# Running the value matmuls of an attention stage as pairs of 64-row matmuls

## The chip, the cores and the metric

The kernel runs on one core of a Trainium2 chip. The metric is the device time of one execution in microseconds; lower is better. The core's engines work side by side, each through its own instructions in order: TensorE (PE, with its weight loads as PEld), VectorE (DVE), ScalarE (ACT), GpSimd (POOL) and SyncE (SP, which here only issues DMAs). They wait for each other by semaphores.

## The reference

There are two stages. The first is an attention without softmax, over 8 batches of 3008 rows with 256 columns, and a key width of 64; the second a feed-forward layer with a cosine gate over the 24064 rows of the first one's result.

```python
scores = (1 / 3008) * z @ z.T             # per batch: [3008, 3008], z is [3008, 64]
attn   = maximum(scores, 0) ** 2
x      = u * (attn @ v)                   # u, v: [3008, 256]
h      = x.reshape(24064, 256) @ w_in     # w_in: [256, 2048]
out    = (h * cos(h)) @ w_out             # w_out: [2048, 256]
```

Everything enters and leaves in float32.

## The kernel before, in words

Inputs are loaded with a cast to float16 (`emit_in_dma`, DMAs issued by POOL). `z` is stored twice side by side, so that its transpose `zTt` holds the same 64 rows in partitions 0 to 63 and 64 to 127. The factors 1/S are taken out of the first stage and put into the second.

**First stage.** The unit of work is a slot: one block of 256 query columns (`IB`, 12 blocks per batch, the last with 192) against four key blocks of 128 rows (`JPG` = 4). A batch has 12 x 6 = 72 slots, the whole stage 576. Slot `s` does the following.

- Scores (L233): four matmuls with a contraction over 64 rows into `scp`, two PSUM banks wide. They come in pairs, one on partitions 0 to 63 and one on 64 to 127, each half of the array with its own bank. `ps_sc` has two such tiles, so the scores of slot s+2 need the relu of slot s.
- Relu from PSUM into `rt` (L245 on ACT for 15 slots of 20, L247 on DVE for the other 5, which follow one another), then the square into `at` (L251 on DVE for 13 of 20, L255 on POOL for 7). Which engine takes which is a fixed pattern in the slot number.
- Values (L271), five slots later (`LAG_SLOTS` = 5): for each of the four key blocks and each half `nh` of the 256 value columns a matmul with a contraction over all 128 key rows, `v16` as the weights and `at` as the moving operand, into `oacc`. One `oacc` tile is one PSUM bank: both `nh` halves of a query block, 2 x 256 float32 columns. It collects six slots; `ps_acc` has two of them.
- After the sixth slot, x is formed (L282): for each `nh`, DVE multiplies the accumulator by the transposed `u` (`uTt`) into `xst`, which SP sends to a DRAM scratch `xT_dram`. There are 96 such query blocks.

Between the slots stand side jobs for the next batch (`side_items_for`): groups of up to eight 128 x 128 transposes of `z` (L137) and of `u` (L152) on PE into a bank `tps` of the pool `ps_tp` (two banks), each copied to SBUF by DVE or ACT in turn (L128, L130), nine groups per batch.

**Second stage.** Blocks of 512 rows: `hps` (L317), cosine on ACT (L325), product on DVE (L328), `ops` (L344), copy on ACT (L351), DMA out. It begins when the first has ended.

The order on each engine is that of a list scheduler that places the instructions at build time, with priorities and the free buffers of the pools in view. What is written later in the program can so stand earlier on an engine, where a buffer is free; a tile from a pool with no free buffer waits for the release of the oldest one.

Of the kernel before, what the change touches and what calls it, by code (L numbers as in the profile page):

```python
# [10 lines left out]
FP16 = mybir.dt.float16  # L11
FP32 = mybir.dt.float32


def _cdiv(a, b):
    return (a + b - 1) // b
# [3 lines left out]
def kernel(  # L20
# [9 lines left out]
    nc = tc.nc  # L30
    AF = mybir.ActivationFunctionType
    ALU = mybir.AluOpType

    B, S, D = u.shape
    dqk = z.shape[2]
    Dff = moe_w_in.shape[1]
    NTOK = B * S
    P = 128

    NJ = _cdiv(S, P)  # L40
    S_pad = NJ * P
    JLAST = S - (NJ - 1) * P
    NDH = _cdiv(D, P)
    NFT = _cdiv(Dff, P)

    IBW = 256
    IB = [(o, min(IBW, S - o)) for o in range(0, S, IBW)]
    JPG = 4
    TPG = 8
# [26 lines left out]
    with tc.tile_pool(name="a_in", bufs=2) as inpool, \  # L76
# [4 lines left out]
            tc.tile_pool(name="a_r", bufs=4) as rpool, \  # L81
            tc.tile_pool(name="a_a", bufs=8) as apool, \
            tc.tile_pool(name="ps_sc", bufs=2, space=bass.MemoryType.PSUM) as ps_sc, \
            tc.tile_pool(name="ps_acc", bufs=2, space=bass.MemoryType.PSUM) as ps_acc, \
            tc.tile_pool(name="ps_tp", bufs=2, space=bass.MemoryType.PSUM) as ps_tp:

        z16s, u16s, v16s, zTs, uTs = {}, {}, {}, {}, {}

# [35 lines left out]
        def tp_copy(dst, src):  # L124
            nonlocal tp_cnt
            tp_cnt += 1
            if tp_cnt % 2 == 0:
                nc.vector.tensor_copy(dst, src)  # L128
            else:
                nc.scalar.copy(dst, src)  # L130

        def emit_tp_z(bb, j0):
            z16 = z16s[bb]
            npk = min(TPG, NJ - j0)
            tps = ps_tp.tile([P, TPG * P], FP16, name="tps")
            for k in range(npk):
                nc.tensor.matmul(  # L137
                    tps[:, k * P:(k + 1) * P],
                    z16[:, j0 + k, :],
                    id16,  # L140
                    is_transpose=True,
                    start=(k == 0),
                    stop=(k == npk - 1),
                )
            tp_copy(zTs[bb][:, j0 * P:(j0 + npk) * P], tps[:, 0:npk * P])

        def emit_tp_u(bb, dh, j0):
            u16 = u16s[bb]
            npk = min(TPG, NJ - j0)
            tps = ps_tp.tile([P, TPG * P], FP16, name="tps")  # L150
            for k in range(npk):
                nc.tensor.matmul(  # L152
                    tps[:, k * P:(k + 1) * P],
                    u16[:, j0 + k, dh * P:(dh + 1) * P],
                    id16,
                    is_transpose=True,
                    start=(k == 0),
                    stop=(k == npk - 1),
                )
            tp_copy(uTs[bb][:, dh, j0 * P:(j0 + npk) * P], tps[:, 0:npk * P])  # L160

        def side_items_for(bb):
            items = []
            nb = bb + 1
            if nb < B:
                if nb >= 2:
                    items.append(lambda n=nb: alloc_zT(n))
                    items.append(lambda n=nb: alloc_uT(n))
                for j0 in range(0, NJ, TPG):
                    items.append(lambda n=nb, j=j0: emit_tp_z(n, j))  # L170
                for dh in range(NDH):
                    for j0 in range(0, NJ, TPG):
                        items.append(lambda n=nb, d=dh, j=j0: emit_tp_u(n, d, j))
                if nb + 1 < B:
                    items.append(lambda n=nb + 1: emit_in_dma(n))
            return items
# [7 lines left out]
        for j0 in range(0, NJ, TPG):  # L184
            emit_tp_z(0, j0)
        alloc_uT(0)
        for dh in range(NDH):
            for j0 in range(0, NJ, TPG):
                emit_tp_u(0, dh, j0)
# [12 lines left out]
        accs = {}  # L202
# [5 lines left out]
        for s in range(nslots + LAG_SLOTS):  # L208
            if s < nslots:
                b, gi, j0 = slots[s]  # L210
                if b != prev_b:
                    prev_b = b
                    while side_q:
                        side_q.pop(0)()
                    items = side_items_for(b)
                    nsb = len(IB) * (NJ // JPG)
                    every = max(1, nsb // (len(items) + 1)) if items else nsb
                    side_tick = 0
                    side_q = items
                    side_every = every  # L220
                side_tick += 1
                if side_q and (side_tick % side_every == 0):
                    side_q.pop(0)()
                ioff, iw = IB[gi]
                ztb = zTs[b]
                scp = ps_sc.tile([P, JPG * IBW], FP32, name="scp")
                nblk = (JPG * IBW * 4) // 2048
                per_blk = JPG // nblk
                for kk in range(per_blk):
                    for blk in range(nblk):  # L230
                        k = blk * per_blk + kk
                        r0 = blk * dqk
                        nc.tensor.matmul(  # L233
                            scp[:, k * IBW:k * IBW + iw],
                            ztb[r0:r0 + dqk, (j0 + k) * P:(j0 + k + 1) * P],
                            ztb[r0:r0 + dqk, ioff:ioff + iw],
                            start=(kk == 0),
                            stop=(kk == per_blk - 1),
                        )
                rt = rpool.tile([P, JPG, IBW], FP16, name="rt")  # L240
                at = apool.tile([P, JPG, IBW], FP16, name="at")
                scv = scp.rearrange("p (k w) -> p k w", k=JPG)
                ew_cnt += 1
                if (ew_cnt * 7919) % 20 < RELU_ACT_OF20:
                    nc.scalar.activation(rt[:, :, 0:iw], scv[:, :, 0:iw], AF.Relu)  # L245
                else:
                    nc.vector.tensor_scalar(  # L247
                        rt[:, :, 0:iw], scv[:, :, 0:iw], 0.0, None, ALU.max
                    )
                if (ew_cnt * 104729) % 20 < SQ_DVE_OF20:  # L250
                    nc.vector.tensor_tensor(  # L251
                        at[:, :, 0:iw], rt[:, :, 0:iw], rt[:, :, 0:iw], ALU.mult
                    )
                else:
                    nc.gpsimd.tensor_tensor(  # L255
                        at[:, :, 0:iw], rt[:, :, 0:iw], rt[:, :, 0:iw], ALU.mult
                    )
                ring[s] = at
            s2 = s - LAG_SLOTS
            if s2 >= 0:  # L260
                b2, gi2, j0_2 = slots[s2]
                ioff2, iw2 = IB[gi2]
                v16 = v16s[b2]
                if j0_2 == 0:
                    accs[(b2, gi2)] = ps_acc.tile([P, NDH * IBW], FP32, name="oacc")
                acc = accs[(b2, gi2)]
                at2 = ring.pop(s2)
                for k in range(JPG):
                    jj = j0_2 + k
                    for nh in range(NDH):  # L270
                        nc.tensor.matmul(  # L271
                            acc[:, nh * IBW:nh * IBW + iw2],
                            v16[:, jj, nh * P:(nh + 1) * P],
                            at2[:, k, 0:iw2],
                            start=(jj == 0 and nh == 0),
                            stop=(jj == NJ - 1 and nh == NDH - 1),
                        )
                if j0_2 + JPG >= NJ:
                    uT16 = uTs[b2]
                    xst = xpool.tile([P, NDH, IBW], FP16, name="xst")  # L280
                    for nh in range(NDH):
                        nc.vector.scalar_tensor_tensor(  # L282
                            xst[:, nh, 0:iw2],
                            acc[:, nh * IBW:nh * IBW + iw2],
                            1.0,
                            uT16[:, nh, ioff2:ioff2 + iw2],
                            ALU.mult,
                            ALU.mult,
                        )
                    del accs[(b2, gi2)]  # L290
                    for nh in range(NDH):
                        nc.sync.dma_start(
                            xT_dram[nh, :, b2 * S + ioff2:b2 * S + ioff2 + iw2],
                            xst[:, nh, 0:iw2],
                        )
# [99 lines left out]
```

## Time and profile before

| | |
|---|---|
| device time, median of 2 runs | 1498.08 us (1497.26 to 1498.9) |
| span of the profiled execution | 1495.1 us |
| TensorE clock granted, mean | 0.992 of full |
| PE, DVE, ACT, POOL busy, share of the span | 97%, 72%, 65%, 31% |
| first value matmul of the stage | 26.8 us |
| last x formed (L282) | 829.6 us |

The profile is that of one execution. A time of its own is not given beside its span; the median of the runs lies 3.0 us above the span, which is what lies around the first and the last instruction. The page has the busy time of each engine, the chain of work that ended last (followed back from the end, with the share of each line in it) and groups of instructions with their mean durations. Answers of the trace add the instructions in order of time (start and duration in us; a row joins several of one kind, "x4"), and who waited for whom. [...]matmuls that follow each other overlap in the records; what counts is the distance between their starts.

### The profile page before, as it was taken

Reading aid. Unit: us, or ns where it says so; the run is one execution under the profiler, and the core shown is the slowest. Engines: PE = TensorE matmul, PEld = TensorE weight load, DVE = VectorE, ACT = ScalarE, POOL = GpSimd, SP = SyncE. Lnnn points to the kernel's source line nnn. Section 1 sums busy time; section 2 is a strip of 40 time slices with the busy share of each in tenths; the row PEclk is TensorE's granted clock in tenths of the full one; section 3 lists DMA queues with packets and bytes.
Section 4 is the critical chain, followed back from the end, with each engine's and each line's share of the span. In section 5 each row is a group of like instructions: output and inputs, shape, how many; then the busy total and the mean of one; then the engine's idle time right before and its main releaser. Section 6 shows DMA issues by size and latency. Waiting matters only on the chain.

```text
span 1495.1 us, 29453 instructions
## 1 busy us (share of the span) xinstructions
PE 1443.2 (97%) x12000; PEld 953.8 (64%) x12000; DVE 1075.4 (72%) x1524; ACT 975.8 (65%) x1409; POOL 467.4 (31%) x274
## 2 busy tenths in 40 slices
PE   3799999999999999999999999999999999999998
PEld 2566666666666666666666666666666666666666
DVE  2487976877878878778677767667667667667664
ACT  1546566566565565665656877777777777778775
POOL 4565655656565554555555000000000000000000
PEclk9799999999999999999999999999999999999999
DMA  9990716434346250000100121121121111111111
GB/s 167 155 129 19 80 20 96 38 59 61 34 67 70 42 74 19 15 18 17 30 19 19 35 64 50 57 64 50 57 63 52 57 60 54 57 59 56 57 57 51
DMA packets 165001, 84.09 MB, mean 56 GB/s; under 512 B 55809, under 2 KB 164609, under 8 KB 164865
## 3 DMA queue, kind: packets, MB, share of 16 engines
q0 software_dynamic: 99616, 32.90, 20.5%
q1 hardware_dynamic: 65248, 49.30, 10.9%
q8 instruction: 94, 1.54, 0.4%
q14 instruction: 43, 0.34, 0.1%
HBM read 78.12 MB, written 36.96 MB: 77 GB/s over the span
## 4 chain that ended last, share of the span: by engine, by line
PE 82%; DVE 10%; DMA 2%; ACT 2%; issue 2%; POOL 0%; DVEq 0%; POOLq 0%; ACTq 0%
PE oacc L271 27%; PE hps L317 22%; PE ops L344 22%; PE scp L233 10%; DVE rt L247 5%; DVE at L251 4%; ACT rt L245 2%; DMA u_122<-in_u_dram 2%; DVE xst L282 1%; PE tps L152 1%; DMA u_106<-in_u_dram 1%; PE tps L137 0%; DVE uTt L128 0%; POOL z_100 L93 0%; ACT uTt L130 0%
## 5 line engine op out<-in xcount | busy, mean ns | idle before, releaser
L245 ACT ACTIVATE rt<-scp 128x1024 f16<-128x1024 f32 (+1 forms) x431 | 429.2, 1006 | 286.6 <-PE scp L233 270.7
L255 POOL TENSOR_TENSOR at<-rt 128x1024 f16<-128x1024 f16 (+1 forms) x202 | 398.5, 1978 | 322.4 <-ACT rt L245 165.7
L251 DVE TENSOR_TENSOR at<-rt 128x1024 f16<-128x1024 f16 (+1 forms) x374 | 372.8, 1006 | 156.6 <-ACT rt L245 154.1
L233 PE MATMUL scp<-zTt 64*128 64x256 f16 (+1 forms) x2304 | 224.5, 273 | 11.0 <-DVE rt L247 8.7
L317 PEld LDWEIGHTS <-w_in_65 128*128 128x128 f16 x1504 | 147.0, 98 | 70.3 <-issue 9.1
L247 DVE TENSOR_SCALAR rt<-scp 128x1024 f16<-128x1024 f32 (+1 forms) x145 | 168.6, 1193 | 1.9 <-PE scp L233 1.7
L351 ACT ACTIVATE osb<-ops 128x256 f32<-128x256 f32 x188 | 71.7, 382 | 147.9 <-PE ops L344 147.9
L233 PEld LDWEIGHTS <-zTt 64*128 64x128 f16 x2304 | 70.1, 94 | 123.9 <-issue 117.0
L282 DVE SCALAR_TENSOR_TENSOR xst<-oacc,uTt 128x256 f16<-128x256 f32 x192 | 74.8, 409 | 12.0 <-PE oacc L271 12.0
L271 PE MATMUL oacc<-at,v_110 128*128 128x256 f16 (+1 forms) x576 | 74.4, 272 | 0.5 <-DVE at L251 0.5
L271 PE MATMUL oacc<-at,v_5547 128*128 128x256 f16 (+1 forms) x576 | 74.2, 272 | 0.0
L271 PE MATMUL oacc<-at,v_6949 128*128 128x256 f16 (+1 forms) x576 | 74.1, 272 | 0.0
L271 PE MATMUL oacc<-at,v_4145 128*128 128x256 f16 (+1 forms) x576 | 74.1, 272 | 0.0
L271 PE MATMUL oacc<-at,v_1341 128*128 128x256 f16 (+1 forms) x576 | 74.1, 272 | 0.0
L271 PE MATMUL oacc<-at,v_2743 128*128 128x256 f16 (+1 forms) x576 | 74.1, 272 | 0.0
L271 PE MATMUL oacc<-at,v_126 128*128 128x256 f16 (+1 forms) x576 | 73.9, 272 | 0.0
L271 PE MATMUL oacc<-at,v_8351 128*128 128x256 f16 (+1 forms) x576 | 73.2, 272 | 0.0
L271 PEld LDWEIGHTS <-v_110 128*128 128x128 f16 x576 | 50.1, 98 | 19.9 <-issue 15.3
L271 PEld LDWEIGHTS <-v_1341 128*128 128x128 f16 x576 | 49.9, 98 | 19.4 <-issue 14.9
L271 PEld LDWEIGHTS <-v_6949 128*128 128x128 f16 x576 | 49.9, 98 | 19.4 <-issue 14.9
L271 PEld LDWEIGHTS <-v_2743 128*128 128x128 f16 x576 | 49.9, 98 | 19.4 <-issue 14.9
L271 PEld LDWEIGHTS <-v_4145 128*128 128x128 f16 x576 | 49.9, 98 | 19.4 <-issue 14.9
(1767 smaller groups left out, 2559.0 us busy)
## 6 DMA issues: line engine op xcount, KB each, us to landing
out_dram<-osb SPq DMA_DIRECT2D x47, 512.0 KB, 2.9
xT_dram<-xst SPq DMA_DIRECT2D x176, 64.0 KB, 1.6
u_106<-in_u_dram POOLq DMA_DIRECT2D x1, 1472.0 KB, 12.7
v_110<-in_v_dram POOLq DMA_DIRECT2D x1, 1472.0 KB, 18.5
u_122<-in_u_dram POOLq DMA_DIRECT2D x1, 1472.0 KB, 23.4
v_126<-in_v_dram POOLq DMA_DIRECT2D x1, 1472.0 KB, 25.7
u_1337<-in_u_dram POOLq DMA_DIRECT2D x1, 1472.0 KB, 14.3
v_1341<-in_v_dram POOLq DMA_DIRECT2D x1, 1472.0 KB, 16.3
```

Of the source, the lines that this page charges most:

```text
L152: nc.tensor.matmul(tps[:, k * P:(k + 1) * P], u16[:, j0 + k, dh * P:(dh + 1) * P], id16, is_transpose=True, start=(k == 0), stop=(k == npk ...
L233: nc.tensor.matmul(scp[:, k * IBW:k * IBW + iw], ztb[r0:r0 + dqk, (j0 + k) * P:(j0 + k + 1) * P], ztb[r0:r0 + dqk, ioff:ioff + iw], start= ...
L245: nc.scalar.activation(rt[:, :, 0:iw], scv[:, :, 0:iw], AF.Relu)
L247: nc.vector.tensor_scalar(rt[:, :, 0:iw], scv[:, :, 0:iw], 0.0, None, ALU.max)
L251: nc.vector.tensor_tensor(at[:, :, 0:iw], rt[:, :, 0:iw], rt[:, :, 0:iw], ALU.mult)
L255: nc.gpsimd.tensor_tensor(at[:, :, 0:iw], rt[:, :, 0:iw], rt[:, :, 0:iw], ALU.mult)
L271: nc.tensor.matmul(acc[:, nh * IBW:nh * IBW + iw2], v16[:, jj, nh * P:(nh + 1) * P], at2[:, k, 0:iw2], start=(jj == 0 and nh == 0), stop=( ...
L282: nc.vector.scalar_tensor_tensor(xst[:, nh, 0:iw2], acc[:, nh * IBW:nh * IBW + iw2], 1.0, uT16[:, nh, ioff2:ioff2 + iw2], ALU.mult, ALU.mult,)
L317: nc.tensor.matmul(hps[:, 0:tw], w_in16[:, k, ft * P:(ft + 1) * P], xt[:, k, 0:tw], start=(k == 0), stop=(k == NDH - 1),)
L344: nc.tensor.matmul(ops[0:m, :], gt[:, ft, tsub * P:tsub * P + m], w_out16[:, ft, :], start=(ft == 0), stop=(ft == NFT - 1),)
L351: nc.scalar.activation(osb[0:m, tsub, :], ops[0:m, :], AF.Copy, bias=0.0, scale=inv_s2,)
```

## The change

The value matmuls are split in two along the contraction. The half `h` = 0 multiplies key rows 0 to 63 of a block and `h` = 1 rows 64 to 127, each into an accumulator bank of its own, so a slot has 16 value matmuls of 64 rows in place of 8 of 128. When x is formed, ACT copies the first accumulator to SBUF (`s0`, float32), DVE adds the second from PSUM (`s1`, float32), and DVE multiplies the sum by `uTt`; each of the three takes both `nh` halves at once (128 x 512). The two pools `ps_acc` and `ps_tp`, two banks each, become one pool `ps_m` of four banks that both accumulators and the transposes draw from.

```diff
@@ -81,8 +81,8 @@
             tc.tile_pool(name="a_r", bufs=4) as rpool, \
             tc.tile_pool(name="a_a", bufs=8) as apool, \
             tc.tile_pool(name="ps_sc", bufs=2, space=bass.MemoryType.PSUM) as ps_sc, \
-            tc.tile_pool(name="ps_acc", bufs=2, space=bass.MemoryType.PSUM) as ps_acc, \
-            tc.tile_pool(name="ps_tp", bufs=2, space=bass.MemoryType.PSUM) as ps_tp:
+            tc.tile_pool(name="a_s", bufs=2) as spool, \
+            tc.tile_pool(name="ps_m", bufs=4, space=bass.MemoryType.PSUM) as ps_m:
 
         z16s, u16s, v16s, zTs, uTs = {}, {}, {}, {}, {}
 
@@ -132,7 +132,7 @@
         def emit_tp_z(bb, j0):
             z16 = z16s[bb]
             npk = min(TPG, NJ - j0)
-            tps = ps_tp.tile([P, TPG * P], FP16, name="tps")
+            tps = ps_m.tile([P, TPG * P], FP16, name="tps", tag="m")
             for k in range(npk):
                 nc.tensor.matmul(
                     tps[:, k * P:(k + 1) * P],
@@ -147,7 +147,7 @@
         def emit_tp_u(bb, dh, j0):
             u16 = u16s[bb]
             npk = min(TPG, NJ - j0)
-            tps = ps_tp.tile([P, TPG * P], FP16, name="tps")
+            tps = ps_m.tile([P, TPG * P], FP16, name="tps", tag="m")
             for k in range(npk):
                 nc.tensor.matmul(
                     tps[:, k * P:(k + 1) * P],
@@ -262,31 +262,41 @@
                 ioff2, iw2 = IB[gi2]
                 v16 = v16s[b2]
                 if j0_2 == 0:
-                    accs[(b2, gi2)] = ps_acc.tile([P, NDH * IBW], FP32, name="oacc")
+                    accs[(b2, gi2)] = [
+                        ps_m.tile([P, NDH * IBW], FP32, name="oacc", tag="m")
+                        for _ in range(2)
+                    ]
                 acc = accs[(b2, gi2)]
                 at2 = ring.pop(s2)
                 for k in range(JPG):
                     jj = j0_2 + k
                     for nh in range(NDH):
-                        nc.tensor.matmul(
-                            acc[:, nh * IBW:nh * IBW + iw2],
-                            v16[:, jj, nh * P:(nh + 1) * P],
-                            at2[:, k, 0:iw2],
-                            start=(jj == 0 and nh == 0),
-                            stop=(jj == NJ - 1 and nh == NDH - 1),
-                        )
+                        for h in range(2):
+                            r0 = h * dqk
+                            nc.tensor.matmul(
+                                acc[h][:, nh * IBW:nh * IBW + iw2],
+                                v16[r0:r0 + dqk, jj, nh * P:(nh + 1) * P],
+                                at2[r0:r0 + dqk, k, 0:iw2],
+                                start=(jj == 0 and nh == 0),
+                                stop=(jj == NJ - 1 and nh == NDH - 1),
+                            )
                 if j0_2 + JPG >= NJ:
                     uT16 = uTs[b2]
                     xst = xpool.tile([P, NDH, IBW], FP16, name="xst")
-                    for nh in range(NDH):
-                        nc.vector.scalar_tensor_tensor(
-                            xst[:, nh, 0:iw2],
-                            acc[:, nh * IBW:nh * IBW + iw2],
-                            1.0,
-                            uT16[:, nh, ioff2:ioff2 + iw2],
-                            ALU.mult,
-                            ALU.mult,
-                        )
+                    s0 = spool.tile([P, NDH, IBW], FP32, name="s0")
+                    s1 = spool.tile([P, NDH, IBW], FP32, name="s1")
+                    a0 = acc[0].rearrange("p (k w) -> p k w", k=NDH)
+                    a1 = acc[1].rearrange("p (k w) -> p k w", k=NDH)
+                    nc.scalar.copy(s0[:, :, 0:iw2], a0[:, :, 0:iw2])
+                    nc.vector.tensor_tensor(
+                        s1[:, :, 0:iw2], a1[:, :, 0:iw2], s0[:, :, 0:iw2], ALU.add
+                    )
+                    nc.vector.tensor_tensor(
+                        xst[:, :, 0:iw2],
+                        s1[:, :, 0:iw2],
+                        uT16[:, :, ioff2:ioff2 + iw2],
+                        ALU.mult,
+                    )
                     del accs[(b2, gi2)]
                     for nh in range(NDH):
                         nc.sync.dma_start(
```

In the changed file the value matmuls stand at L276, the copy at L290, the sum at L291 and the product at L294; lines up to L262 are where they were.

## The prediction

> **What bounds the kernel now.** I read the page first: the engine shares, then the chain that ended last.
>
> ```profile
> PE 1443.2 (97%) x12000; PEld 953.8 (64%) x12000; DVE 1075.4 (72%) x1524; ACT 975.8 (65%) x1409; POOL 467.4 (31%) x274
> ...
> PE oacc L271 27%; PE hps L317 22%; PE ops L344 22%; PE scp L233 10%; DVE rt L247 5%; DVE at L251 4%; ACT rt L245 2%; DMA u_122<-in_u_dram 2%; DVE xst L282 1%; PE tps L152 1%; DMA u_106<-in_u_dram 1%; PE tps L137 0%; DVE uTt L128 0%; POOL z_100 L93 0%; ACT uTt L130 0%
> ```
>
> TensorE carries the chain, and 38% of the span on it (oacc 27, scp 10, tps 1) is in the attention stage, up to about 830 us. The second stage (hps, ops) is untouched. But DVE rt and DVE at are on the chain too, with 9%: VectorE is second in line. The timeline of TensorE shows the rhythm of a slot (columns: start, duration, what):
>
> ```profile
> 403.95 0.39 PE L233 MATMUL scp<-zTt 64*128 64x256 f16 x4
> 404.27 1.05 PE L271 MATMUL oacc<-at,v_2743 128*128 128x256 f16 x8
> 405.25 0.39 PE L233 MATMUL scp<-zTt 64*128 64x256 f16 x4
> 405.58 1.05 PE L271 MATMUL oacc<-at,v_2743 128*128 128x256 f16 x8
> 406.46 0.61 PE L152 MATMUL tps<-id_58,u_4141 128*128 128x128 f16 x8
> ```
>
> A slot is 1.30 us. One matmul is recorded at 275 ns, so the eight full ones (1.05) start (1.05 - 0.275) / 7 = 0.11 us apart. The four 64-row ones end after 0.39: their last start is at 0.39 - 0.275 = 0.115, so two ran together, then two more, one step of 0.115 apart. Ten steps of 0.109 would make 1.09; the other 0.21 lies where the kinds meet: last scp start 404.07 to first oacc 404.27, and last oacc start 405.05 to next scp 405.25, 0.20 each instead of 0.11. The view of waits counts the same gaps on the weight loads:
>
> ```profile
> PEld L271 <- issue: 118.1, 569, 0.7
> PEld L233 <- issue: 117.0, 540, 2.0
> ...
> PE scp L233 <- DVE rt L247: 8.7, 19, 2.0
> ```
>
> About 0.21 per gap, once per slot each way, with no releaser that the profile knows; and TensorE hardly waits for VectorE (8.7 us in all). So changing between full and half matmuls costs about 0.2 us x 576 slots = 115 us, and the elementwise engines are just fast enough for 1.30. How just, the timeline of VectorE shows where five slots in a row have their relu on it (L247):
>
> ```profile
> 564.15 0.69 DVE L251 TENSOR_TENSOR at<-rt 128x1024 f16<-128x1024 f16 x1 [0.39 <-ACT rt L245]
> 564.76 2.35 DVE L247 TENSOR_SCALAR rt<-scp 128x1024 f16<-128x1024 f32 x2
> 567.02 0.68 DVE L251 TENSOR_TENSOR at<-rt 128x1024 f16<-128x1024 f16 x1
> 567.62 1.22 DVE L247 TENSOR_SCALAR rt<-scp 128x1024 f16<-128x1024 f32 x1
> 568.76 0.41 DVE L282 SCALAR_TENSOR_TENSOR xst<-oacc,uTt 128x256 f16<-128x256 f32 x1
> 569.09 0.92 DVE L251 TENSOR_TENSOR at<-rt 128x1024 f16<-128x1024 f16 x1
> 569.93 0.41 DVE L282 SCALAR_TENSOR_TENSOR xst<-oacc,uTt 128x256 f16<-128x256 f32 x1
> 570.26 2.34 DVE L247 TENSOR_SCALAR rt<-scp 128x1024 f16<-128x1024 f32 x2
> ```
>
> From 564.15 to 572.60 VectorE is never idle, and TensorE waits there once for 0.53 us. This stretch sets what a faster TensorE is worth.
>
> **What the Trainium skill says.** "TensorEngine Tiling (Array Packing)", section "Key Properties", says that changing the tiling mode drains the engine, and that tiles of one mode run in parallel: the trace agrees, with 0.20 instead of 0.11 us at each change and the four scp matmuls in 0.39. "PSUM — Partial Sum Buffer", section "Specifications (TRN2)", says that a VectorE instruction takes at most one tensor input from PSUM; hence the copy of one half to SBUF before the sum; nothing in this trace tests it. "SBUF — State Buffer", section "Who interferes with whom", says that a VectorE instruction with two SBUF inputs contends with GpSimd reading SBUF. The trace agrees: the squares (L251, two SBUF inputs) take 0.68 alone but 1.03 on average, the relus (one PSUM input) 1.21 always.
>
> **The change, part by part.** Instruction order is from the two built programs. Profiled span 1495.1, median of the runs 1498.1: I add 3.0 us to any span.
>
> TensorE. Per slot 8 full matmuls become 8 pairs of halves. Both kinds are now 64-row, so the two changes of mode go and the slot is ten steps: 1.10 at 0.110 a step. Its bounds are 1.09, and 1.20 if every pair takes the 0.115 to 0.12 seen at a first step. That is 0.20 x 576 = 115 us off, if nothing else is late. The 72 groups of 8 transposes stay full matmuls; each used to add 0.45 (with oacc before it in the same mode) and now brings two changes: 0.65, or +14 us.
>
> Start. Before, the nine transpose groups of batch 1 all stand ahead of the second value slot, and TensorE waits for loads from 29 to 56 us:
>
> ```profile
> 28.75 0.39 PE L233 MATMUL scp<-zTt 64*128 64x256 f16 x4
> 42.68 2.80 PE L137 MATMUL tps<-id_58,z_116 128*128 128x128 f16 x24 [13.54 <-DMA z_116<-in_z_dram]
> 50.29 1.89 PE L152 MATMUL tps<-id_58,u_122 128*128 128x128 f16 x16 [4.81 <-DMA u_122<-in_u_dram]
> ...
> 55.86 1.26 PE L271 MATMUL oacc<-at,v_110 128*128 128x256 f16 x10
> ```
>
> With one shared pool of four banks only the first group stands there; the value matmuls can go on at 43.5. That is 12 us won, 8 x 0.65 = 5 paid later: -7.
>
> x, 96 times. Out: two L282 of 0.41, VectorE 0.82. In: on ScalarE a copy 128x512, 0.60 by the line through 256 columns (0.382, L351) and 1024 (1.02, L245). On VectorE the sum from PSUM, 512 columns: 0.69 from 0.41 at 256 and 1.21 at 1024. Then a product of two SBUF inputs at one element a cycle: 0.69 by the same slope; "VectorE: DVE Perf Modes" prices an fp32 two-tensor sum of 512 at 691 ns. Beside GpSimd up to 1.36 (the mean of squares wholly beside it); I take 0.95. VectorE gets 1.64 for 0.82 each, +79 us in all; ScalarE +57. Two instructions overlap by some 0.08, which I take off below.
>
> The relu stretch. Let the first score matmul of the five VectorE slots start at 0, with the next wanted at 1.10, 2.20 and so on. The square ahead of the first relu waits for the last ScalarE relu: -1.10 + 0.39 + 1.02, then 0.6, so VectorE starts at about 1.0. The new order is relu, square, relu, relu, square, sum, relu, product, relu: 1.14 + 0.60 + 2.28 + 0.95 + 0.54 + 1.14 + 0.70 + 1.14 (sum and product weighted by how often they fall inside), and 0.15 for a transpose copy. That ends at 9.65. Scores have two buffers, so the seventh score matmul waits for the fifth relu: six slots take 9.7. Before they took 6 x 1.30 + 0.45 + 0.4 = 8.65 (563.96 to 572.83 in this piece: 8.87).
>
> The other 14 of 20 slots. ScalarE does 0.93 a relu, 2.3 copies of 0.5 for the sum, one transpose copy: 1.07 a slot; TensorE 1.10; with their jitter 1.12. 14 x 1.12 = 15.7, and 1.75 transposes x 0.65 = 1.1.
>
> Bank waits. The accumulators take two of four banks and a transpose takes the third, so after a transpose a new pair needs a bank of the pair that has just ended. In the built order 26 of 96 groups wait there for the copy on ScalarE (about 0.6 after the next scores) and 12 for the sum on VectorE (about 1.4); 26 x 0.6 + 12 x 1.4 = 32 us. Behind that matmul stand TensorE's next slots. A third falls in the relu stretch, where TensorE is late anyway; 0.7 per 20 slots remain.
>
> Sum per 20 slots: before 20 x 1.303 + 2.5 x 0.45 + 0.4 = 27.6; after 9.7 + 15.7 + 1.1 + 0.7 = 27.2. Times 28.5 such cycles: -11; start -7: -18. 1498.1 - 18 = **1480**. So the 115 us are nearly all given back: what is late next is VectorE's relu stretch, then the bank waits.
>
> **Rivals.**
> 1. Clearly faster: the stretch stays at 8.65 (sum and product fall in VectorE's idle time) and bank waits vanish in it: 8.65 + 14 x 1.10 + 1.1 = 25.15; -2.45 x 28.5 - 7 = -77: 1421. For it: VectorE is at 75 to 84% in the windows of this stage. Against: the built order puts the sum and product between the relus.
> 2. Slower, by the pairs themselves: 64-row pairs are seen only two in a row at full clock, with half the instructions per us that ten need. Two weight loads a pair, not hidden, make a step longer. Every 0.01 in a step costs 0.1 x 14 x 28.5 = 40 us in the 14 slots alone; from 0.122 on the kernel is slower than before by 2%. At 0.14 (slot 1.40): +56 for the slots, +14 transposes, +15 bank waits, -11 waits gone, -7 start: 1565. Against: both halves of a pair load within 0.11 us in scp.
> 3. Slower, by VectorE: GpSimd's squares cover the stretch, every square and product takes 1.36: +1.6 per cycle, +46: 1526.
>
> **How the numbers follow.** Forecast 0.45 (own range 1455 to 1510), first rival 0.20, second 0.15, third 0.20. Range 1425 to 1550, leaving out the far ends of the first and second. A measurement here tells about 2% (1468 to 1528). Faster: the first rival and the forecast's low edge, 0.28; slower: the larger part of the second and third, 0.27; same 0.45.
>
> **What would show it.** Right: no issue gaps left between scp and oacc, slots of 1.10 where ScalarE does the relus, a large wait of scp for DVE rt (some 40 us or more, from 8.7), a wait of oacc for the copy and the sum, value matmuls running by 44 us, L294 near 0.95. Wrong: steps of over 0.115 in the pairs; scp waiting for VectorE no more than before; a slot still at 1.30.

## The result, and the profile after

The changed kernel takes 1511.0 us (median of 2 runs, 1510.67 to 1511.33) against 1498.08: a ratio of 1.0089, with a 95% interval of 1.006 to 1.0118. It is slower, by less than 2% but beyond the noise; the forecast was 1480, a gain. The profiled execution spans 1508.8 us (1495.1 before). TensorE's granted clock was lower in it (mean 0.977, against 0.992), but the other run of the changed kernel had 0.986 and took no less (1511.33), so the clock doesn't look like the cause.

First the page of the changed kernel: engine shares, then the chain that ended last.

```profile
PE 1370.6 (91%) x16608; PEld 1076.0 (71%) x16608; DVE 1202.3 (80%) x1524; ACT 1008.9 (67%) x1505; POOL 475.9 (32%) x274
...
PE hps L327 22%; PE ops L354 22%; PE oacc L276 12%; DVE at L251 10%; DVE rt L247 9%; ACT rt L245 4%; PE scp L233 4%; DVE xst L294 3%; DVE s L291 2%; DMA z<-in_z_dram 2%; DMA u<-in_u_dram 1%; PE tps L152 1%; PE tps L137 0%; ACT s L290 0%; DVE uTt L128 0%
```

The second stage still holds 44% of the chain. In the first one the chain has moved: the value matmuls fall from 27% to 12%, and VectorE (at, rt, xst, s) rises from 10% to 24%. The view of waits says where the two meet:

```profile
PEld L233 <- issue: 110.3, 111, 2.6
...
PE scp L233 <- DVE rt L247: 88.4, 90, 2.4
...
PEld L276 <- issue: 15.9, 16, 2.9
...
PE oacc L276 <- DVE at L251: 9.2, 6, 2.7
...
PE oacc L276 <- ACT s L290: 1.3, 1, 1.3
```

The 0.21 us gaps between scores and values, 569 and 540 before, are down to 16 and 111. Those that are left are longer (110.3 us for the 111): most of them lie beside the waits of the score matmuls, the others at transposes. From the last score matmul to the first value matmul the median step is now 0.09 us, and back again 0.11, where both were 0.20. In place of the gaps the score matmuls wait 88.4 us for VectorE's relus, 8.7 before. The timeline of TensorE shows both kinds of slot:

```profile
406.61 0.38 PE L233 MATMUL scp<-zTt 64*128 64x256 f16 x4
406.83 1.04 PE L276 MATMUL oacc<-at,v 64*128 64x256 f16 x16
407.77 0.40 PE L233 MATMUL scp<-zTt 64*128 64x256 f16 x4
407.99 1.05 PE L276 MATMUL oacc<-at,v 64*128 64x256 f16 x16
409.63 0.39 PE L233 MATMUL scp<-zTt 64*128 64x256 f16 x4 [0.59 <-DVE rt L247]
...
424.00 0.38 PE L233 MATMUL scp<-zTt 64*128 64x256 f16 x4
424.21 1.04 PE L276 MATMUL oacc<-at,v 64*128 64x256 f16 x16
425.09 0.38 PE L233 MATMUL scp<-zTt 64*128 64x256 f16 x4
425.31 1.04 PE L276 MATMUL oacc<-at,v 64*128 64x256 f16 x16
426.18 0.38 PE L233 MATMUL scp<-zTt 64*128 64x256 f16 x4
```

Undisturbed, a slot is 1.09 us (424.00 to 425.09 to 426.18): ten steps of 0.109. The score matmul at 409.63 is one of those held up by a relu on VectorE.

**A measure used below.** The trace has all 2304 score matmuls, four to a slot, so each slot has a start. For the 27 whole cycles of 20 slots behind the first I averaged two pieces of time: from the first of the five slots with VectorE relus over six slots ("six"), and the other fourteen ("rest"). Lateness is the time from the start of that first slot to VectorE's first relu; its mean takes in the last cycle too, which is cut short.

| kernel | time us | six us | rest us | lateness us |
|---|---|---|---|---|
| before | 1498.1 | 8.60 | 18.47 | 0.89 |
| changed | 1511.0 | 10.96 | 16.80 | 2.13 |

The rest won 1.67 us per cycle, the six slots lost 2.36. Times 28.5 cycles that is +20; the start gave back 9 (the eighth slot begins at 48.7 us in place of 57.6). That makes +11; the medians say +13.

What makes VectorE late is seen in the piece just ahead of these relus. VectorE in the changed kernel, then GpSimd over the same time:

```profile
395.19 1.35 DVE L294 TENSOR_TENSOR xst<-s,uTt 128x512 f16<-128x512 f32 x1
396.46 4.70 DVE L251 TENSOR_TENSOR at<-rt 128x1024 f16<-128x1024 f16 x2
401.08 0.68 DVE L128 COPY uTt<-tps 128x1024 f16<-128x1024 f16 x1
401.68 1.78 DVE L251 TENSOR_TENSOR at<-rt 128x1024 f16<-128x1024 f16 x1
403.38 0.68 DVE L291 TENSOR_TENSOR s<-oacc,s 128x512 f32<-128x512 f32 x1
404.09 0.69 DVE L294 TENSOR_TENSOR xst<-s,uTt 128x512 f16<-128x512 f32 x1
404.70 1.89 DVE L251 TENSOR_TENSOR at<-rt 128x1024 f16<-128x1024 f16 x3
406.51 1.21 DVE L247 TENSOR_SCALAR rt<-scp 128x1024 f16<-128x1024 f32 x1
```

```profile
394.09 1.89 POOL L255 TENSOR_TENSOR at<-rt 128x1024 f16<-128x1024 f16 x1 [4.12 <-ACT rt L245]
396.42 4.19 POOL L255 TENSOR_TENSOR at<-rt 128x1024 f16<-128x1024 f16 x2 [0.43 <-ACT rt L245]
400.96 1.94 POOL L255 TENSOR_TENSOR at<-rt 128x1024 f16<-128x1024 f16 x1 [0.36 <-ACT rt L245]
```

Beside two squares of GpSimd (4.19 us), two of VectorE's take 4.70 instead of 1.3. The rows join two instructions each; here is the second of each kind alone:

```profile
398.78 2.38 DVE L251 TENSOR_TENSOR at<-rt 128x1024 f16<-128x1024 f16 x1
398.27 2.34 POOL L255 TENSOR_TENSOR at<-rt 128x1024 f16<-128x1024 f16 x1
```

VectorE's square ends at 401.16, 0.55 us after GpSimd's (400.61). Most of the long ones do so in this trace: of VectorE's 124 squares that took over 1.2 us, 115 end 0.54 to 0.57 us after a square of GpSimd ends. From 395.19 to the first relu at 406.51 VectorE is never idle: it is working off a backlog. Over the whole stage its squares took 1006 ns on average before and 1122 now, and the new products 1022 (the first line is of the kernel before; behind the bar stand the busy time and the mean of one):

```profile
L251 DVE TENSOR_TENSOR at<-rt 128x1024 f16<-128x1024 f16 (+1 forms) x374 | 372.8, 1006 | 156.6 <-ACT rt L245 154.1
...
L251 DVE TENSOR_TENSOR at<-rt 128x1024 f16<-128x1024 f16 (+1 forms) x374 | 410.6, 1122 | 52.5 <-ACT rt L245 49.0
...
L294 DVE TENSOR_TENSOR xst<-s,uTt 128x512 f16<-128x512 f32 x96 | 98.1, 1022 | 2.2
```

### The profile page after: what moved, and what is told of

Read it like the earlier page. It is cut to its first block, busy times and chain, and to the rows that moved or that the text cites. A ratio compares the mean times of both kernels' runs of the same rounds, so it can differ in the third digit from the quotient of the medians.

```text
span 1508.8 us, 38747 instructions
## 1 busy us (share of the span) xinstructions
PE 1370.6 (91%) x16608; PEld 1076.0 (71%) x16608; DVE 1202.3 (80%) x1524; ACT 1008.9 (67%) x1505; POOL 475.9 (32%) x274
## 3 DMA queue, kind: packets, MB, share of 16 engines
q8 instruction: 130, 2.13, 0.6%
## 4 chain that ended last, share of the span: by engine, by line
PE 61%; DVE 25%; issue 7%; ACT 5%; DMA 2%; POOL 1%; DVEq 0%; ACTq 0%; POOLq 0%
PE hps L327 22%; PE ops L354 22%; PE oacc L276 12%; DVE at L251 10%; DVE rt L247 9%; ACT rt L245 4%; PE scp L233 4%; DVE xst L294 3%; DVE s L291 2%; DMA z<-in_z_dram 2%; DMA u<-in_u_dram 1%; PE tps L152 1%; PE tps L137 0%; ACT s L290 0%; DVE uTt L128 0%
## 5 line engine op out<-in xcount | busy, mean ns | idle before, releaser
L276 PE MATMUL oacc<-at,v 64*128 64x256 f16 (+1 forms) x9216 | 610.1, 272 | 12.6 <-DVE at L251 9.2
L338 DVE SCALAR_TENSOR_TENSOR gt<-hps,c 128x512 f16<-128x512 f32 x752 | 458.3, 680 | 191.5 <-ACT c L335 190.5
L276 PEld LDWEIGHTS <-v 64*128 64x128 f16 x9216 | 488.1, 96 | 40.0 <-issue 15.9
L251 DVE TENSOR_TENSOR at<-rt 128x1024 f16<-128x1024 f16 (+1 forms) x374 | 410.6, 1122 | 52.5 <-ACT rt L245 49.0
L335 ACT ACTIVATE c<-hps,pihalf 128x512 f16<-128x512 f32 x752 | 448.8, 702 | 2.2
L354 PE MATMUL ops<-w_out,gt 128*128 128x256 f16 x3008 | 428.5, 273 | 0.0
L327 PE MATMUL hps<-xt,w_in 128*128 128x512 f16 x1504 | 417.1, 379 | 1.5 <-DVE gt L338 1.5
L354 PEld LDWEIGHTS <-gt 128*128 128x128 f16 x3008 | 294.2, 98 | 149.9
L233 PE MATMUL scp<-zTt 64*128 64x256 f16 (+1 forms) x2304 | 229.6, 273 | 90.0 <-DVE rt L247 88.4
L233 PEld LDWEIGHTS <-zTt 64*128 64x128 f16 x2304 | 117.8, 95 | 123.3 <-issue 110.3
L327 PEld LDWEIGHTS <-w_in 128*128 128x128 f16 x1504 | 146.9, 98 | 70.5 <-issue 9.3
L290 ACT COPY s<-oacc 128x512 f32<-128x512 f32 x96 | 55.6, 579 | 109.7 <-PE oacc L276 109.6
L294 DVE TENSOR_TENSOR xst<-s,uTt 128x512 f16<-128x512 f32 x96 | 98.1, 1022 | 2.2
L291 DVE TENSOR_TENSOR s<-oacc,s 128x512 f32<-128x512 f32 x96 | 64.1, 668 | 11.6 <-ACT s L290 9.3
## 6 DMA issues: line engine op xcount, KB each, us to landing
u<-in_u_dram POOLq DMA_DIRECT2D x8, 1472.0 KB, 13.5
```

The costliest lines, as they stand in the source:

```text
L233: nc.tensor.matmul(scp[:, k * IBW:k * IBW + iw], ztb[r0:r0 + dqk, (j0 + k) * P:(j0 + k + 1) * P], ztb[r0:r0 + dqk, ioff:ioff + iw], start= ...
L251: nc.vector.tensor_tensor(at[:, :, 0:iw], rt[:, :, 0:iw], rt[:, :, 0:iw], ALU.mult)
L276: nc.tensor.matmul(acc[h][:, nh * IBW:nh * IBW + iw2], v16[r0:r0 + dqk, jj, nh * P:(nh + 1) * P], at2[r0:r0 + dqk, k, 0:iw2], start=(jj == ...
L291: nc.vector.tensor_tensor(s1[:, :, 0:iw2], a1[:, :, 0:iw2], s0[:, :, 0:iw2], ALU.add)
L294: nc.vector.tensor_tensor(xst[:, :, 0:iw2], s1[:, :, 0:iw2], uT16[:, :, ioff2:ioff2 + iw2], ALU.mult,)
L327: nc.tensor.matmul(hps[:, 0:tw], w_in16[:, k, ft * P:(ft + 1) * P], xt[:, k, 0:tw], start=(k == 0), stop=(k == NDH - 1),)
```

## Experiments

Four theories. **A:** VectorE's load sets the pace, by its amount. **B:** the burst of five relus in a row with two score buffers. **C:** the bank waits of the shared pool. **D** (formed after the first four runs): VectorE, which takes its instructions in order, reaches its relus late, because squares and products with two SBUF inputs stand still beside GpSimd ahead of them; TensorE then waits. Intervals are of the ratio to the kernel before.

**a1_relu_spread.** In the changed kernel:

```diff
-                if (ew_cnt * 7919) % 20 < RELU_ACT_OF20:
+                if ew_cnt % 4 != 0:
```

> The changed kernel with the five VectorE relus of 20 slots spread out, every fourth slot, in place of five in a row; the number of relus and squares on each engine stays. Theory A (VectorE's whole load: it is busy 93 to 95% of the stage, so the load sets the pace wherever it lies): within 1% of the changed kernel, 1500 to 1512 us. Theory B (the burst: five relus in a row with two score buffers make TensorE wait, and between bursts the time isn't won back): the wait of scp for DVE rt falls from 88 us to under 30 and the time to 1455 to 1475. Theory C (bank waits of the shared pool): no change, 1505 to 1512.

Measured: 1540.3 us, ratio 1.0281 (1.0266 to 1.0297). No theory had this: slower than the changed kernel by 29 us. Waits of this kernel:

```profile
PE scp L233 <- DVE rt L247: 129.2, 95, 6.4
```

The five relus of a cycle start on average 1.2 to 2.7 us after their first score matmul (2.1 to 3.0 in the changed kernel, 0.9 to 1.7 before), so they are still late, and TensorE now waits for longer (129 us, not 88). So B is wrong as put: spreading the burst doesn't help. A is wrong as put too: with the same work on each engine the place of the relus changed the time by 1.9%. That in a burst the delay of an engine already behind is shared by five slots would explain it, but this is only argued; the grown wait is what the run shows.

**a2_relu17.** `RELU_ACT_OF20 = 17` in place of 15.

> The changed kernel with 17 of 20 relus on ScalarE in place of 15 (three in a row on VectorE). Takes 2 x 1.13 us off VectorE in every 20 slots and puts 2 x 0.93 on ScalarE. Theory A (VectorE's load): -2.3 x 28.5 = -64 at most, 1445 to 1465. Theory B (the burst): about as much, since the burst shrinks by two. Theory C (bank waits): under 10 us, 1500 to 1512.

Measured: 1469.6 us, ratio 0.9811 (0.9796 to 0.9826): -41 us against the changed kernel. C is out as the main cause; A and B aren't told apart, and the gain is a little under what both expected (1445 to 1465).

**a3_no_product.**

```diff
                     nc.vector.tensor_tensor(
-                        s1[:, :, 0:iw2], a1[:, :, 0:iw2], s0[:, :, 0:iw2], ALU.add
-                    )
-                    nc.vector.tensor_tensor(
-                        xst[:, :, 0:iw2],
-                        s1[:, :, 0:iw2],
-                        uT16[:, :, ioff2:ioff2 + iw2],
-                        ALU.mult,
+                        xst[:, :, 0:iw2], a1[:, :, 0:iw2], s0[:, :, 0:iw2], ALU.add
                     )
```

> The changed kernel without the product with u: the sum on VectorE writes x itself (left out: the factor u). Takes 96 x 0.95 = 91 us off VectorE; the banks are released as before, by the copy and the sum. Theory A (VectorE's load): 1420 to 1450. Theory B (the burst): only what falls inside the bursts counts, 0.7 of 3.4 products, so some 20 us: about 1490. Theory C (bank waits): no change.

Measured: 1473.2 us, ratio 0.9836 (0.9821 to 0.985): -38. That is twice what B expected (some 20) and well short of A (61 to 91): 98 us of VectorE work gone, 38 us won. VectorE isn't simply full.

**b1_shared_pool.** The kernel before with one pool, from which the accumulator and the transposes then draw:

```diff
-            tc.tile_pool(name="ps_acc", bufs=2, space=bass.MemoryType.PSUM) as ps_acc, \
-            tc.tile_pool(name="ps_tp", bufs=2, space=bass.MemoryType.PSUM) as ps_tp:
+            tc.tile_pool(name="ps_m", bufs=4, space=bass.MemoryType.PSUM) as ps_m:
...
```

> The kernel before with the shared pool of four banks alone; full matmuls, one accumulator, x formed as before. By the prediction's start term: value matmuls run from 44 us and not from 56, eight transpose groups come back later at 0.45: -12 + 4 = -8, about 1490. If the shared pool itself cost much (Theory C), it would be slower than before.

Measured: 1492.65 us, ratio 0.9964 (0.995 to 0.9978): -5.3, where -8 was expected. The start term holds nearly, and the shared pool as such costs nothing there. Its value matmuls, in the timeline of TensorE:

```profile
42.83 1.01 PE L136 MATMUL tps<-id,z 128*128 128x128 f16 x8 [14.36 <-DMA z<-in_z_dram]
43.63 1.91 PE L270 MATMUL oacc<-at,v 128*128 128x256 f16 x8
```

**d1_no_pool_squares.**

```diff
-            tc.tile_pool(name="a_r", bufs=4) as rpool, \
+            tc.tile_pool(name="a_r", bufs=8) as rpool, \
...
-                    nc.gpsimd.tensor_tensor(
-                        at[:, :, 0:iw], rt[:, :, 0:iw], rt[:, :, 0:iw], ALU.mult
-                    )
+                    at = rt
```

> The changed kernel with GpSimd's seven squares of 20 slots left out (there the relu's result goes unsquared into the value matmuls). Theory D (VectorE arrives late at its relus, because its squares and products, with two SBUF inputs, stand still while GpSimd squares): L251 and L294 all at 0.68 to 0.70, the wait of scp for DVE rt below 30 us, 1395 to 1425. Theory A (VectorE's load by its count of instructions alone): the count is the same, so 1490 to 1512.

Measured: 1439.3 us, ratio 0.9609 (0.9594 to 0.9623): -72. Two of its groups (mean of one behind the bar), and a wait:

```profile
L251 DVE TENSOR_TENSOR at<-rt 128x1024 f16<-128x1024 f16 (+1 forms) x374 | 252.6, 679 | 145.1 <-ACT rt L245 138.5 <-PE oacc L274 2.9
...
L292 DVE TENSOR_TENSOR xst<-s,uTt 128x512 f16<-128x512 f32 x96 | 65.0, 677 | 2.2
```

```profile
PE scp L233 <- DVE rt L247: 56.3, 77, 1.9
```

Squares fall from 1122 to 679 ns and products from 1022 to 677: that they are slow is GpSimd's doing. The first relu is 1.26 us late (2.13 in the changed kernel), and six slots take 9.40. D is right that this slowness adds to the backlog, but not in size: the time is 14 us over its range, since TensorE still waits 56 us. Without GpSimd's squares, too, VectorE with five relus doesn't follow a TensorE at 1.09. Not all of the 72 us need come from VectorE's faster squares: 6 us lie ahead of the whole cycles (the first of them begins at 60.5 us, not 66.6), and this kernel also spares the value matmuls the wait for GpSimd's squares and gives `rt` eight buffers. No run separates these.

**d2_sum_in_psum.** The sum is written over the second accumulator, and the product reads it there.

```diff
...
-                        s1[:, :, 0:iw2], a1[:, :, 0:iw2], s0[:, :, 0:iw2], ALU.add
+                        a1[:, :, 0:iw2], a1[:, :, 0:iw2], s0[:, :, 0:iw2], ALU.add
...
-                        s1[:, :, 0:iw2],
+                        a1[:, :, 0:iw2],
```

> The changed kernel with the sum written back into its PSUM bank, so that the product has one SBUF input and one from PSUM. Theory D (standing still beside GpSimd): L294 at 0.69 in place of 1.02 and the time down by 25 to 35 us, 1475 to 1487. Theory C (banks): the second bank is held 0.7 us longer, so slower, 1515 to 1525. If only counts matter (Theory A): no change, 1505 to 1515.

Measured: 1490.5 us, ratio 0.9951 (0.9936 to 0.9965): -20. Group of the product:

```profile
L293 DVE TENSOR_TENSOR xst<-oacc,uTt 128x512 f16<-128x512 f32 x96 | 64.8, 675 | 2.2
```

675 ns in place of 1022, and none over 692, with GpSimd about as busy (its squares take 400.5 us, 409.5 in the changed kernel): with one SBUF input the product doesn't stand still. The gain is somewhat under D's range (the first relu is 1.88 us late), and C's loss doesn't appear.

**d3_pairs_alone** and **d4_x_alone.** The change in two halves. The first is the changed kernel with before's x formed from `acc[1]`; the second the kernel before with the new way of forming x from its one accumulator (`a0` and `a1` both views of `acc`).

```diff
...
-                    nc.scalar.copy(s0[:, :, 0:iw2], a0[:, :, 0:iw2])
...
+                        nc.vector.scalar_tensor_tensor(
+                            xst[:, nh, 0:iw2],
+                            acc[1][:, nh * IBW:nh * IBW + iw2],
...
```

> The matmul part alone: 64-row pairs into two banks as in the changed kernel, but x formed as before from the second bank (left out: the first half of the sum). VectorE has before's work again. If the pairs were free to run at 1.09 a slot: 1498 - 115 + 14 - 7 = 1390. Theory D: VectorE is then less late but not on time, 1435 to 1460. Theory C (bank waits): half the releases are as before, 1480 to 1500.

> The x part alone: the kernel before with its full matmuls and one accumulator, x formed by a copy, a sum and a product (the one accumulator taken for both halves, so x comes out doubled). VectorE gets 87 us more in a stage in which it was at 78%. If the slot of 1.30 covers it: 1498 to 1506. Theory D (the relus get late): 1510 to 1530.

Measured: pairs alone 1475.2 us, ratio 0.9852 (0.9835 to 0.9868), so -23; x alone 1514.05, ratio 1.0107 (1.0092 to 1.0122), so +16 (within D's range). Pairs alone are worse than D expected. A wait of that kernel:

```profile
PE scp L233 <- DVE rt L247: 73.1, 75, 2.0
```

Even with before's work on VectorE, TensorE at 1.09 runs into the relus (six slots 10.18, lateness 1.69). The time is near C's range (1480 to 1500), but TensorE waits there 8.1 us in all for what the value matmuls need, and nearly all of that for squares, not for banks. And the halves don't add: -23 + 16 = -7, measured +13. The same x costs 16 us behind a slow TensorE and 36 behind a fast one.

**The last four** take VectorE's relus away: `RELU_ACT_OF20` is 18 or 20, with and without the sum in PSUM, and 20 in the kernel before as the comparison.

> The changed kernel with 18 of 20 relus on ScalarE (two in a row on VectorE) and the sum kept in PSUM. By Theory D (VectorE late at its relus) both steps add: 1511 - 41 - 20 from the runs of each, and the third relu moved another 15: 1430 to 1450.

> The changed kernel with all relus on ScalarE and the sum kept in PSUM. No relu stands on VectorE, so it can't be late there; ScalarE then needs 20 x 0.93 + 3.3 x 0.5 + 1.25 x 0.92 = 21.4 us per 20 slots against TensorE's 22 plus transposes. Theory D: 24.2 to 25 per 20 slots in place of 27.8, so -80 to -100: 1410 to 1432. If ScalarE becomes the bound (its copy waits for the last value matmul with the next relus behind it): 1440 to 1470.

> The changed kernel with all relus on ScalarE, x formed as in the change. Theory D: the product's standing still beside GpSimd no longer holds up a relu, so it costs little: within 10 us of the same with the sum in PSUM, 1415 to 1440. Theory A (VectorE's load): 15 to 20 us above that one.

> The kernel before with all relus on ScalarE. TensorE sets its pace at 1.30 a slot and waits for VectorE's relus 8.7 us in all: 1485 to 1495. It tells how much of a gain of the last three kernels belongs to the pairs and how much to the relus alone.

| kernel | time us | ratio (95%) | six us | rest us |
|---|---|---|---|---|
| e1_relu18_psum | 1447.85 | 0.9671 (0.9656 to 0.9685) | 9.01 | 16.54 |
| e2_relu20_psum | 1394.06 | 0.9308 (0.9294 to 0.9321) | 7.03 | 16.64 |
| e3_relu20 | 1407.56 | 0.9397 (0.9381 to 0.9413) | 7.11 | 17.00 |
| e4_before_relu20 | 1482.53 | 0.9902 (0.9888 to 0.9917) | 7.97 | 18.62 |

Only e1 fell inside its range. e3 lies below its own, and 13.5 us above e2, between what D (within 10) and A (15 to 20) expected; e4 gained a little more than expected from the relus alone. With all relus on ScalarE the same change wins 75 us (e4 to e3), and with the sum in PSUM 88 (e4 to e2). e2 is 6.9% faster than the kernel before. Busy time of the engines in two stretches of 100 us, e1 and then e2 (PE, PEld, DVE, ACT, POOL):

```profile
500.00:600.00 100.00, 92.43 (x1632) 81.99 (x1628) 79.16 (x92) 76.53 (x89) 56.71 (x30) 0.98 0.19 35
```

```profile
500.00:600.00 100.00, 99.95 (x1813) 90.25 (x1813) 79.34 (x92) 94.03 (x106) 60.54 (x31) 1.00 0.08 22
```

VectorE is busy 79% in both, and e1 is 54 us slower. So VectorE is full in neither, and against A it isn't its amount of work that sets the pace; the two relus of 20 that stand in its queue do harm while a fifth of its time is free. (They are 69 us of work too; only a1 moved relus without changing the amount.) As for the slow product: its groups hold 120.9 us in e3 and 65.1 in e2, and it costs 13.5 us where VectorE has no relus, 0.24 us for each us that it is longer. With relus there, 98.1 against 64.8 us (changed kernel to d2) costs 20.5, or 0.62 for each. e2 came out below its range (1410 to 1432), at 23.67 us per cycle where 24.2 was the least expected.

## Why the prediction was wrong

By its steps:

- Step of a pair: right. 0.110 was taken, ten steps run at 0.109; rival 2 is out.
- Start: nearly right. -7 was forecast, -5.3 measured for the pool alone; in the changed kernel the eighth slot begins 8.9 us earlier.
- The added operations: nearly right. Copy 0.58 (0.60 forecast), sum 0.67 (0.69, though the line through 0.41 and 1.21 gives 0.68), product 1.02 (0.95).
- The other 14 slots: 16.80 measured, 15.7 + 1.1 + 0.7 = 17.5 forecast, so 0.7 better; about 0.3 of it are the shorter slots of the blocks of 192 columns (last point).
- Bank waits: oversized. 32 us were forecast before hiding. TensorE is idle ahead of value matmuls for 12.6 us in all, most of it for squares; 1.3 for the copy and 0.9 for a copy of transposes are the only waits for a bank that the view of waits names.
- VectorE's own time in the relu stretch: right. From first relu to fifth 8.69 measured, 8.64 summed.
- **The failed step:** "VectorE starts at about 1.0". (Its terms give 0.91, and before it was 0.89.) It starts at 2.13, so the six slots took 10.96, not 9.7: 1.26 more per cycle. I let VectorE enter the stretch with only one square to do, and its work in the other 14 slots is nowhere summed in my working. There it was busy 88% of the time (69% before). The squares grew from 1006 to 1122 ns (+38 us in all), the products stood still too, and both lie in the queue ahead of the relus. Two runs show the shares in part: with before's work on VectorE the faster pairs alone bring the lateness to 1.69 (d3), and without GpSimd's squares it falls from 2.13 to 1.26 (d1).
- The price of GpSimd, of use for the product and for rival 3, was too low as well. My 1.36 was called the mean of squares wholly beside GpSimd; it is that of squares at least half beside it. By the same measure the changed kernel has 1.78.
- A term on the other side: my cycle of before, 27.6, was 0.5 too long (8.60 + 18.47 = 27.07). I had taken every slot at 1.30. The blocks of 192 columns make five slots in 72 shorter by 0.05, one by 0.26 and five by 0.21: 0.43 per 20 slots.

The cycle after is thus 1.26 - 0.70 = 0.56 longer than forecast and the cycle before 0.53 shorter. Times 28.5 that is 31 us, and 1480 + 31 = 1511; that it meets the measured time to the microsecond is luck, since the start is off by 1 to 2 us as well. The nearest case was rival 3 (1526, "GpSimd's squares cover the stretch"): right on the engine and on GpSimd, but wrong on the place. It looked inside the stretch; the delay was gathered ahead of it.

What was expected of the profile of the changed kernel came mostly true: hardly any issue gaps of the old kind, slots of 1.09, a scp wait of 40 us or more (88), value matmuls from 44 us (43.8), L294 near 0.95. The wait of the value matmuls for the copy and the sum did not: 1.3 us for the one, none for the other. The mechanism was right as far as the place where TensorE is held up; but it doesn't give a sign when gain and loss are each near 100 us.

## What to carry to other kernels

Before making the leading engine faster, sum the work of the second one over a whole cycle, at the durations that it has beside its neighbours, and ask how late its queue reaches the instructions that the leading engine waits for; a busy share tells little of that (VectorE's was 79% in the same 100 us of two kernels that are 54 us apart). Take what the leading engine needs soonest (here the relus, with two score buffers) off an in-order queue that can stand still: the same change made the kernel 0.9% slower with five relus there and 5.1% faster (e4 to e3) with none. And beside a busy GpSimd, an operand of a VectorE product left in PSUM can be cheaper than one kept in SBUF (675 ns against 1022).

## What the runs showed of the hardware that I had not expected

- Two VectorE squares of 0.68 us took 4.70 us beside two GpSimd squares that followed each other. GpSimd's lose little (4.19 against 2 x 1.89 alone), while each of VectorE's stood still until the GpSimd square beside it had ended and ended 0.55 us later. In the changed kernel 115 of the 124 squares over 1.2 us and 35 of the 40 products over 1.0 us end that way.
- In d2 an in-place sum in PSUM takes 0.68 us and the product from PSUM that follows it 0.68, whether a square of GpSimd runs beside them or not (none took over 0.70).
- Spreading the relus evenly was 1.9% slower than having five in a row (1540.3 / 1511.0). Why stays open: the waits of TensorE grew, but the order that the scheduler made on every engine differs too, and no run separates the two.
